# First loads of a gated mix of linear attention and a SwiGLU network: one weight piece moved to another queue, another held behind a memset, and the tables of GpSimd cut into tasks

## The chip, the core and the metric

The kernel runs on one core of a Trainium2 chip. The metric is the device time of one execution in microseconds (us); the median of several runs is given with their lowest and highest. A profiled execution has a time of its own and a span, which is the stretch from the first to the last recorded instruction.

## What is computed

For 2048 tokens of width 640 (bf16), a linear attention with 32 heads of width 20 and a SwiGLU network of width 1728 are computed from the same x and mixed by a gate for each token:

```python
g = sigmoid((x * gate_w).sum(-1, keepdims=True))
q, k, v = split_heads(x @ wqkv)                  # 32 heads of 20
pq, pk  = q @ w_phi[h], k @ w_phi[h]
phi     = concat(softmax(p), softmax(-p))        # for q and for k, 40 wide
kv, z   = phi_k^T v, sum of phi_k over tokens
a       = (phi_q kv) / (phi_q z + 1e-6) @ wo
b       = (silu(x @ w_gate) * (x @ w_up)) @ w_down
out     = g * a + (1 - g) * b
```

## The kernel before

The tokens are handled in four blocks of 512 (bt) and 16 tiles of 128 (t). x is loaded transposed into xT, five column blocks of 128 each. The SwiGLU width is cut into 14 pieces k of 128: for a block and a k, five matmuls with w_gate and five with w_up fill two PSUM banks ("gate", "up"); ACT takes a tanh of the first into hT and a copy of the second into one of three us buffers, DVE combines, and POOL multiplies hT by us ("hmul"), which frees the us buffer. w_phi is folded into the weights of q and k: POOL builds a block diagonal table wbd from w_phi (build_wbd, lines 507 to 519: five times a copy and two selects), PE multiplies wqT by wbd ("pre", premult, line 692), and ACT copies the result to wqk ("prev"). POOL also builds a mask kvm (build_mask, lines 521 to 532), which the kv sums need much later.

The order of work isn't written out by hand. Each piece of work is a task with an engine, a cost, dependences and a rank (prio); class _Plan (line 225) runs a small clock and, whenever an engine is free, emits the task with the lowest rank whose dependences are met. A transfer has a due time written in the source (land), and tasks that need it are emitted after this time. So due times set the order in which each engine's instructions stand, and the engines keep that order: an instruction that waits holds up those behind it. Real waits are on semaphores that the tracker (line 33) places from overlaps of reads and writes. A transfer waits only for what it reads and writes in SBUF, and is issued in the order of its engine's list.

The head (ffn_head, line 602) is the first real work of PE: after nine warm-up matmuls on zeros (warm, line 537) it computes k = 0 and k = 1 of block 0 side by side, 20 matmuls in four bank halves. It goes by column blocks of x (0 and 1, then 2, 3, 4), each with w_gate and then with w_up, so that it can start when the first columns are there. Behind it come k = 2 and 3 of block 0, then k = 0, 1, 2 of block 1, then the five premultiplies for k's weights.

The first transfers: on SP's list x's first block in four transposing transfers (line 476), then w_gate and w_up columns 256 to 511 (load_gu, line 449), x's second block, and so on through all weights (lines 479 to 493); on ACT's list w_gate and w_up columns 0 to 255 (lines 477, 478), behind the load of the activation table and a tanh of one element; on POOL's list w_phi (line 473). Small memsets of DVE (zeros for the warm-up, ones in v for the denominators, zero rows of hT and wd) are at lines 498 to 505. All matmuls carry line 395, all activations line 405, transfers line 423.

Of the kernel before, what the change touches and what calls it, by code (L numbers as in the profile page):

```python
# [6 lines left out]
P = 128  # L7
S_TOK = 2048
D = 640
# [289 lines left out]
def _build(  # L299
# [116 lines left out]

    out_evs = []

    def dma(eng, dst, src, transpose=False, keep=False):
        eobj = tr.engobj[eng]  # L420
        reads = [src] if src.tensor.name in tr.addr else []
        writes = [dst] if dst.tensor.name in tr.addr else []
        fn = (lambda: eobj.dma_start(dst, src, transpose=True)) if transpose else (lambda: eobj.dma_start(dst, src))
        ev = run(eng, fn, reads=reads, writes=writes, semname="dma")
        if keep:
            out_evs.append(ev)

    chain = {}  # L430

    def load(eng, dst, src, land, prio, transpose=False, name="load", cost=0.06):

        t = add(eng, cost, lambda: dma(eng, dst, src, transpose=transpose), prio=prio, lat=2.0, name=name)
        t.land = land
        t.after = chain.get(eng)
        chain[eng] = t
        return t

    def rows(a):  # L440
        return a.rearrange("(c p) j -> p c j", p=P)
# [12 lines left out]
    def load_x(bt, prio, *cuts):  # L454

        tok = slice(512 * bt, 512 * bt + 512)
        out_ = []
        for i, (c0, c1, land) in enumerate(cuts):
            out_ += [load("sp", xT[:, c0:c1, tok], x2[tok, c0 * P:c1 * P], land, prio + 0.1 * i, True, "x%d" % bt)] * (c1 - c0)
        return out_  # L460
# [7 lines left out]
    def load_gate():  # L468
        with nc.allow_non_contiguous_dma(reason="gate_w column load (640 elems)"):
            dma("act", wvg[:, :, D:D + 1], gate_ap)  # L470
    gw_l = add("act", 0.5, load_gate, prio=-7, lat=6.0, name="gw")
    gw_l.hold = 11.0
    ph_l = load("pool", wph[:, :, :], rows(A_w_phi.rearrange("h e f -> (h e) f")), 6.0, -20, cost=0.9)

    xs = [None] * NBT
    xs[0] = load_x(0, -42, (0, 2, 4.2), (2, 3, 6.7), (3, 4, 7.3), (4, 5, 7.8))
    wgl[0] = load("act", wg[:, :, 0:256], gsrc[:, :, 0:256], 5.1, -19, cost=0.5)
    wul[0] = load("act", wu[:, :, 0:256], usrc[:, :, 0:256], 6.2, -18, cost=0.5)
    load_gu(1, "sp", (8.9, 10.0), -37)
    xs[1] = load_x(1, -36, (0, 5, 13.2))  # L480
    load_gu(2, "sp", (15.0, 16.2), -35)
    wkT_l = load_wT(1, 19.2, -34)
    load_gu(3, "sp", (22.6, 24.5), -33)
    wv_l = load("sp", wvg[:, :, 0:D], rows(A_wqkv[:, 2 * D:3 * D]), 28.6, -32)
    xs[2] = load_x(2, -31, (0, 5, 30.5))
    load_gu(4, "sp", (32.4, 34.3), -30)
    wgl[NPC] = load("sp", wg[:, :, 1664:1728], gsrc[:, :, 1664:1728], 33.8, -29)
    wul[NPC] = load("sp", wg[:, :, 1728:1792], usrc[:, :, 1664:1728], 34.1, -28)
    xs[3] = load_x(3, -27, (0, 5, 38.0))
    wqT_l = load_wT(0, 41.5, -26)  # L490
    wd_l = [load("sp", wd[:, 0:13, :], rows(B_w_down[0:13 * P, :]), 52.0, -25),
            load("sp", wd[0:64, 13, :], B_w_down[13 * P:F_FFN, :], 53.0, -24)]
    wo_l = load("sp", wo[:, :, :], rows(A_wo), 56.0, -23)
    xl = [x_[4] for x_ in xs]

    zero = add("dve", 0.3, lambda: memset(us[:, 0, :], 0.0, "dve"), prio=-20, name="zero")
    table = add("act", 1.3, lambda: actop(us[:, 1, 0:1], us[:, 0, 0:1], ACTF.Tanh), deps=[zero], prio=-20, name="table")
    wgl[0].deps.append(table)  # L500
    v1ones = v1[:, :, :].rearrange("p t (h d) -> p t h d", d=DH + 1)[:, :, :, DH:DH + 1]
    ones_t = add("dve", 0.4, lambda: memset(v1ones, 1.0, "dve"), prio=-19)
    add("dve", 1.0, lambda: memset(hT[64:P, :, 13, :], 0.0, "dve"), prio=-18)
    wdz = add("dve", 0.7, lambda: memset(wd[64:P, 13, :], 0.0, "dve"), prio=-18)
    wd_l[1].deps.append(wdz)

    def build_wbd():
        for c in range(5):
            nh = PHI_NH[c]
            d_ = wbd[:, c, 0:nh, :]  # L510
            s_ = wph[:, c, :].unsqueeze(1).to_broadcast([P, nh, DH])
            poolop(lambda d_=d_, s_=s_: pool.tensor_copy(d_, s_), [wph[:, c, :]], [d_])
            poolop(lambda d_=d_, c=c, nh=nh: pool.affine_select(
                out=d_, in_=d_, pattern=[[-DH, nh], [0, DH]], compare_op=ALU.is_ge, fill=0.0,
                base=P * c - DH * PHI_H0[c], channel_multiplier=1), [d_], [d_])
            poolop(lambda d_=d_, c=c, nh=nh: pool.affine_select(
                out=d_, in_=d_, pattern=[[DH, nh], [0, DH]], compare_op=ALU.is_gt, fill=0.0,
                base=DH * PHI_H0[c] + DH - P * c, channel_multiplier=-1), [d_], [d_])
    wbd_t = add("pool", 6.0, build_wbd, deps=[ph_l], prio=-5, name="wbd")

    def build_mask():
        memset(kvm[:, :, :], 0.0, "pool")
        for g in range(5):
            d_ = kvm[:, g, :].rearrange("p (k d) -> p k d", d=DH + 1)
            memset(d_, 1.0, "pool")
            poolop(lambda d_=d_, g=g: pool.affine_select(
                out=d_, in_=d_, pattern=[[-2 * DH, 4], [0, DH + 1]], compare_op=ALU.is_ge, fill=0.0,
                base=P * g - 2 * DH * WHEAD[g], channel_multiplier=1), [d_], [d_])
            poolop(lambda d_=d_, g=g: pool.affine_select(
                out=d_, in_=d_, pattern=[[2 * DH, 4], [0, DH + 1]], compare_op=ALU.is_gt, fill=0.0,  # L530
                base=2 * DH * WHEAD[g] + 2 * DH - P * g, channel_multiplier=-1), [d_], [d_])
    mask_t = add("pool", 5.0, build_mask, prio=-6, name="mask")


    wctx = {}
# [66 lines left out]
    def ffn_head():  # L602
        tsl = slice(0, 512)
        cs = [{}, {}]
        before = warm_t
        lasts = [None, None]
        for c0, c1 in ((0, 2), (2, 3), (3, 4), (4, 5)):
            for j, (w, wl) in enumerate(((wg, wgl), (wu, wul))):
                def fn(c0=c0, c1=c1, j=j, w=w):
                    mms([(bank(cs[k]["ps"], j, 0, 512), w[:, c, P * k:P * k + P], xT[:, c, tsl], c == 0, c == 4)  # L610
                         for c in range(c0, c1) for k in range(2)])
                last = add("pe", _mm(*[512] * (2 * (c1 - c0))), fn, deps=[xs[0][c1 - 1], wl[0]], prio=-5,
                           acq=[("ps", cs[0], "ps"), ("ps", cs[1], "ps")] if c0 == 0 and j == 0 else (), name="head")
                last.after = before
                before = last
                lasts[j] = last
        for k in range(2):
            ffn_tail(0, k, cs[k], lasts, 0)

# [72 lines left out]
    def premult(which, wT_l, prio, step=0.0, at=0.0):  # L692
        ev = []
        for m in range(5):
            ctx = {}

            def fn(m=m, ctx=ctx):
                i = ctx["ps"]
                l = [wqT[:, 5 * which + c, P * m:P * m + P] for c in range(5)]

                def r(c, k0, k1):
                    return wbd[:, c, k0:k1, :].rearrange("p k f -> p (k f)")
                mms([(bank(i, 0, 0, 140), l[0], r(0, 0, 7), True, False),
                     (bank(i, 0, 120, 260), l[1], r(1, 0, 7), False, False),
                     (bank(i, 0, 240, 320), l[2], r(2, 0, 4), False, True),
                     (bank(i, 1, 0, 80), l[2], r(2, 4, 8), True, False),
                     (bank(i, 1, 60, 200), l[3], r(3, 0, 7), False, False),
                     (bank(i, 1, 180, 320), l[4], r(4, 0, 7), False, True)])
            t1 = add("pe", 0.4, fn, deps=[wT_l, wbd_t], prio=prio + step * m, acq=[("ps", ctx, "ps")], name="pre")
            t1.hold = at + 1.1 * m if at else 0.0  # L710

            def ev_fn(m=m, ctx=ctx):
                i_ = wide(ctx["ps"], 1024).rearrange("p (b x) -> p b x", b=2)[:, :, 0:320]
                o_ = wqk[:, which, m, :].rearrange("p (b x) -> p b x", b=2)
                actop(o_, i_, ACTF.Copy)
            ev.append(add("act", 0.6, ev_fn, deps=[t1], prio=-1, rel=[("ps", ctx, "ps")], name="prev"))
        return ev
# [102 lines left out]
    def kvpart(bt, half, prio):  # L820
# [28 lines left out]
        if bt == NBT - 1:  # L849
            ks = kvsb[:, half, :, :].rearrange("p g w -> p (g w)")  # L850
            km = kvm[:, :, :].rearrange("p g w -> p (g w)")
            kvs_t[half] = add("dve", 0.75, lambda: dveop(lambda: dve.tensor_tensor(ks, ka, km, ALU.mult), [ka, km], [ks]),
                              deps=[e_, mask_t], prio=1.4, name="kvs")
    kva_t = {}
    kvs_t = {}

# [134 lines left out]
```

## Time and profile before

| | |
|---|---|
| median of 3 runs | 292.27 us (291.34 to 293.55) |
| profiled execution | 292.22 us, span 290.5 us |
| PE busy | 282.6 us |
| DVE busy | 218.3 us |
| POOL busy | 165.3 us |
| ACT busy | 146.3 us |
| granted TensorE clock | 1.00 |

Times in the profile count from the start of the span. An engine's name with a q (SPq, ACTq) is its queue of instructions, here the issue of transfers; the number behind the start is how long the issue took, not the transfer. In square brackets stands how long the engine was idle before, and what released it. "x4" are four instructions merged into a row; PE's matmuls overlap, so a row's length is from the first start to the last end. In the list of waits, a row gives the sum of the waits, their number and the longest.

### The profile page before, as it was taken

How to read it: one execution, taken by the hardware profiler on the slowest of the kernel's cores; microseconds unless marked ns; L12 is line 12 of the kernel's file. 1: busy time of each engine (PE TensorE's matmuls, PEld its weight loads, DVE VectorE, ACT ScalarE, POOL GpSimd, SP SyncE). 2: the span in 40 equal slices, each digit the busy share in tenths (PEclk: the TensorE clock that was granted, in tenths of full speed). 3: DMA queues.
4: the chain of work that ended last, by engine and by line, in shares of the span. 5: the costliest groups of instructions: out<-in, count | busy, mean ns of one | idle time of the engine just before them, and what ended most of it. 6: DMA issues, size and time to landing. Idle time of an engine off the chain costs nothing.

```text
span 290.5 us, 5068 instructions
## 1 busy us (share of the span) xinstructions
PE 282.6 (97%) x1980; PEld 152.8 (53%) x2017; DVE 218.3 (75%) x323; ACT 146.3 (50%) x216; POOL 165.3 (57%) x136
## 2 busy tenths in 40 slices
PE   6899999999999999999999999999999999999996
PEld 2345555555555456556555556554556554554554
DVE  1232979999999998978998895899997879641022
ACT  2457567656746644443455335555663554654200
POOL 7764164763964686455647555767886546644300
PEclk9999999999999999999999999999999999999999
DMA  7999998000000000000326553434433543121021
GB/s 152 248 238 319 246 262 271 2 2 2 0 0 2 0 2 0 2 0 14 73 49 95 113 63 75 115 69 90 85 76 71 90 93 68 21 54 20 23 70 45
DMA packets 62776, 23.38 MB, mean 80 GB/s; under 512 B 51280, under 2 KB 62752, under 8 KB 62752
## 3 DMA queue, kind: packets, MB, share of 16 engines
q1 hardware_dynamic: 60752, 22.37, 34.7%
q10 hardware_dynamic: 1968, 0.66, 1.2%
q8 instruction: 16, 0.26, 0.4%
q14 instruction: 8, 0.07, 0.1%
q0 software_dynamic: 32, 0.03, 0.0%
HBM read 8.30 MB, written 2.62 MB: 38 GB/s over the span
## 4 chain that ended last, share of the span: by engine, by line
PE 95%; DMA 2%; issue 1%; ACT 1%; DVE 0%
PE ps L395 95%; DMA wu<-in_B_w_up_dram 2%; ACT L405 0%; ACT wqk L405 0%; ACT us L405 0%; DVE xsb L651 0%
## 5 line engine op out<-in xcount | busy, mean ns | idle before, releaser
L809 POOL TENSOR_TENSOR phi<-phi,rc 128x1280 bf16<-128x1280 bf16 x32 | 75.8, 2368 | 53.4 <-DVE rc L803 53.4
L579 POOL TENSOR_TENSOR hT<-hT,us 128x512 bf16<-128x512 bf16 (+1 forms) x56 | 64.3, 1154 | 45.0 <-DVE hT L573 30.3
L395 PE MATMUL ps<-xT,wg 128*128 128x512 bf16 x266 | 67.0, 379 | 1.7 <-DMA xT<-in_A_x_dram 1.0
L395 PE MATMUL ps<-xT,wu 128*128 128x512 bf16 x260 | 64.9, 379 | 1.0 <-DMA wu<-in_B_w_up_dram 1.0
L395 PE MATMUL ps<-wd,hT 128*128 128x128 bf16 (+1 forms) x440 | 62.1, 298 | 0.4
L573 DVE SCALAR_TENSOR_TENSOR hT<-hT,ps 128x512 bf16<-128x512 bf16 (+1 forms) x56 | 37.8, 676 | 26.4 <-ACT hT L405 26.4
L405 ACT ACTIVATE hT<-ps 128x512 bf16<-128x512 f32 (+1 forms) x56 | 33.4, 597 | 45.6 <-PE ps L395 45.3
L799 DVE TENSOR_REDUCE sm<-phi 128x64 f32<-128x1280 bf16 x32 | 47.3, 1479 | 11.5 <-ACT phi L405 11.5
L405 ACT ACTIVATE phi<-phi 128x1280 bf16<-128x1280 bf16 x32 | 40.6, 1269 | 21.5 <-DVE phi L789 21.2
L395 PEld LDWEIGHTS ps<-wd,hT 128*128 128x128 bf16 x448 | 35.0, 98 | 27.9
L395 PE MATMUL ps<-wqk,xT 128*128 128x128 bf16 (+1 forms) x311 | 47.4, 297 | 0.5
L405 ACT ACTIVATE us<-ps 128x512 bf16<-128x512 f32 (+1 forms) x56 | 33.3, 598 | 21.8 <-PE ps L395 21.6
L395 PEld LDWEIGHTS ps<-xT,wu 128*128 128x128 bf16 x260 | 25.3, 98 | 32.0 <-DMA wu<-in_B_w_up_dram 1.5
L395 PEld LDWEIGHTS ps<-xT,wg 128*128 128x128 bf16 x280 | 25.6, 98 | 26.3 <-DMA wg<-in_B_w_gate_dram 1.9
L395 PEld LDWEIGHTS ps<-wqk,xT 128*128 128x128 bf16 x320 | 26.4, 98 | 22.0
L777 DVE TENSOR_REDUCE mx<-ps 128x32 f32<-128x640 f32 x32 | 26.0, 811 | 7.7 <-PE ps L395 7.7
L781 DVE TENSOR_REDUCE mn<-ps 128x32 f32<-128x640 f32 x32 | 25.8, 808 | 0.0
L789 DVE TENSOR_TENSOR phi<-mn,ps 128x640 bf16<-128x640 f32 x32 | 25.7, 803 | 0.0
L785 DVE TENSOR_TENSOR phi<-ps,mx 128x640 bf16<-128x640 f32 x32 | 25.4, 795 | 0.0
L395 PE MATMUL ps<-wo,oT 128*128 128x128 bf16 (+1 forms) x158 | 23.7, 298 | 0.1
L395 PE MATMUL ps<-wvg,xT 128*128 128x129 bf16 (+1 forms) x156 | 22.6, 298 | 0.2
L665 POOL TENSOR_TENSOR xsb<-xsb,xb 128x640 bf16<-128x640 bf16 x12 | 16.7, 1396 | 9.1 <-ACT xb L405 9.1
(42 smaller groups left out, 174.8 us busy)
## 6 DMA issues: line engine op xcount, KB each, us to landing
out_dram<-xsb SPq DMA_DIRECT2D x15, 160.0 KB, 1.8
wd<-in_B_w_down_dram SPq DMA_DIRECT2D x1, 2080.0 KB, 9.8
wvg<-in_A_wqkv_dram SPq DMA_DIRECT2D x1, 800.0 KB, 7.6
wo<-in_A_wo_dram SPq DMA_DIRECT2D x1, 800.0 KB, 10.6
wg<-in_B_w_gate_dram SPq DMA_DIRECT2D x2, 320.0 KB, 4.2
wu<-in_B_w_up_dram SPq DMA_DIRECT2D x2, 320.0 KB, 4.9
wg<-in_B_w_gate_dram SPq DMA_DIRECT2D x1, 640.0 KB, 4.5
wu<-in_B_w_up_dram SPq DMA_DIRECT2D x1, 640.0 KB, 5.9
```

The costliest lines, as they stand in the source:

```text
L395: last = pe.matmul(o, lhsT=l, rhs=r, start=st, stop=sp_, skip_group_check=True)
L405: run("act", lambda: act.activation(o, i, func, scale=scale), reads=reads, writes=[o])
L573: dveop(lambda: dve.scalar_tensor_tensor(out=hap, in0=hap, scalar=1.0, in1=g_, op0=ALU.add, op1=ALU.mult), [hap, g_], [hap])
L579: poolop(lambda: pool.tensor_tensor(hap, hap, u_, ALU.mult), [hap, u_], [hap])
L665: poolop(lambda: pool.tensor_tensor(x_, x_, b_, ALU.add), [x_, b_], [x_])
L777: dveop(lambda: dve.tensor_reduce(a, b, AX.X, ALU.max), [b], [a])
L781: dveop(lambda: dve.tensor_reduce(a, b, AX.X, ALU.min), [b], [a])
L785: dveop(lambda: dve.tensor_tensor(o_, a, b, ALU.subtract), [a, mx[:, ctx["st"], :]], [o_])
L789: dveop(lambda: dve.tensor_tensor(o_, a, b, ALU.subtract), [b, mn[:, ctx["st"], :]], [o_])
L799: dveop(lambda: dve.tensor_reduce(a, b, AX.X, ALU.add), [b], [a])
L809: poolop(lambda: pool.tensor_tensor(a, a, b, ALU.mult), [a, r], [a])
```

## The change

Transfers: w_up columns 0 to 255 and w_phi move to SP's list; x's first block is loaded in two transfers (columns blocks 0 and 1, and 2 to 4) instead of four; w_gate columns 0 to 255 stay alone on ACT's list, and the transfer is entered as reading the ones of v, so that it waits for DVE's memset of them (behind). SP's list now begins: x blocks 0 and 1, x blocks 2 to 4, w_up 0 to 255, w_gate and w_up 256 to 511, w_phi, x's second block, and then as before. The due times of the loads are rewritten.

The head takes w_gate first, column blocks 0 and 1, then 2 to 4, and then ten matmuls with w_up over all five. The number of matmuls and their operands stay the same.

wbd and the mask become five tasks each, one for each of the five parts, with the same copy or memset and two selects; the memset of the whole mask to zero goes. The mask's rank falls from -6 to 3, but while POOL waits for w_phi's due time nothing else is ready, and all five parts of the mask stand ahead of wbd in POOL's list; all of wbd stands ahead of the first hmul, as before. With the new due times the order of the later tasks changes in places: the same groups, some exchanged with neighbours (on PE for example a v tile stands ahead of a gate and up pair, and some kv, num and down groups change places).

```diff
-    def dma(eng, dst, src, transpose=False, keep=False):
+    def dma(eng, dst, src, transpose=False, keep=False, behind=()):
+
         eobj = tr.engobj[eng]
-        reads = [src] if src.tensor.name in tr.addr else []
+        reads = ([src] if src.tensor.name in tr.addr else []) + list(behind)
...
-    ph_l = load("pool", wph[:, :, :], rows(A_w_phi.rearrange("h e f -> (h e) f")), 6.0, -20, cost=0.9)
-
     xs = [None] * NBT
-    xs[0] = load_x(0, -42, (0, 2, 4.2), (2, 3, 6.7), (3, 4, 7.3), (4, 5, 7.8))
-    wgl[0] = load("act", wg[:, :, 0:256], gsrc[:, :, 0:256], 5.1, -19, cost=0.5)
-    wul[0] = load("act", wu[:, :, 0:256], usrc[:, :, 0:256], 6.2, -18, cost=0.5)
-    load_gu(1, "sp", (8.9, 10.0), -37)
-    xs[1] = load_x(1, -36, (0, 5, 13.2))
-    load_gu(2, "sp", (15.0, 16.2), -35)
-    wkT_l = load_wT(1, 19.2, -34)
...
+    xs[0] = load_x(0, -42, (0, 2, 4.2), (2, 5, 7.0))
+    wgl[0] = add("act", 0.5, lambda: dma("act", wg[:, :, 0:256], gsrc[:, :, 0:256], behind=[v1ones]), prio=-19, name="load")
+    wgl[0].land = 5.4
+    wul[0] = load("sp", wu[:, :, 0:256], usrc[:, :, 0:256], 8.0, -39)
+    load_gu(1, "sp", (9.4, 10.5), -37)
+    ph_l = load("sp", wph[:, :, :], rows(A_w_phi.rearrange("h e f -> (h e) f")), 10.9, -36.5)
+    xs[1] = load_x(1, -36, (0, 5, 13.0))
+    load_gu(2, "sp", (15.0, 16.5), -35)
+    wkT_l = load_wT(1, 19.6, -34)
...
     ones_t = add("dve", 0.4, lambda: memset(v1ones, 1.0, "dve"), prio=-19)
+    wgl[0].deps += [table, ones_t]
...
-    wbd_t = add("pool", 6.0, build_wbd, deps=[ph_l], prio=-5, name="wbd")
-
-    def build_mask():
-        memset(kvm[:, :, :], 0.0, "pool")
-        for g in range(5):
...
-    mask_t = add("pool", 5.0, build_mask, prio=-6, name="mask")
...
+    wbd_t = [add("pool", 1.2, lambda c=c: build_wbd(c), deps=[ph_l], prio=-5, name="wbd") for c in range(5)]
+
+    def build_mask(g):
...
+    mask_t = [add("pool", 1.0, lambda g=g: build_mask(g), prio=3, name="mask") for g in range(5)]
...
-        lasts = [None, None]
-        for c0, c1 in ((0, 2), (2, 3), (3, 4), (4, 5)):
-            for j, (w, wl) in enumerate(((wg, wgl), (wu, wul))):
+        lasts = []
+        for j, (w, wl) in enumerate(((wg, wgl), (wu, wul))):
+            for c0, c1 in ((0, 2), (2, 5)) if j == 0 else ((0, 5),):
...
-                lasts[j] = last
+            lasts.append(last)
...
-            t1 = add("pe", 0.4, fn, deps=[wT_l, wbd_t], prio=prio + step * m, acq=[("ps", ctx, "ps")], name="pre")
+            t1 = add("pe", 0.4, fn, deps=[wT_l] + wbd_t, prio=prio + step * m, acq=[("ps", ctx, "ps")], name="pre")
```

The other due times that change lie 0.5 to 3.4 us earlier (w_v 28.6 to 26.3, x's fourth block 38.0 to 36.8, w_o 56.0 to 52.6, for example), but for w_up columns 512 to 767 and w_k, which lie 0.3 and 0.4 later.

More of the change, by code (lines that the diff above doesn't have):

```diff
@@ L426, in dma @@
             out_evs.append(ev)
+    v1ones = v1[:, :, :].rearrange("p t (h d) -> p t h d", d=DH + 1)[:, :, :, DH:DH + 1]
     chain = {}
@@ L482, in _build @@
-    wkT_l = load_wT(1, 19.2, -34)
[L483 to L492, printed above, removed]
@@ L493, in _build @@
-    wo_l = load("sp", wo[:, :, :], rows(A_wo), 56.0, -23)
+    xs[0] = load_x(0, -42, (0, 2, 4.2), (2, 5, 7.0))
[5 more added lines that the diff above has]
+    xs[1] = load_x(1, -36, (0, 5, 13.0))
@@ new lines, in _build @@
+    load_gu(2, "sp", (15.0, 16.5), -35)
+    wkT_l = load_wT(1, 19.6, -34)
+    load_gu(3, "sp", (22.0, 24.0), -33)
+    wv_l = load("sp", wvg[:, :, 0:D], rows(A_wqkv[:, 2 * D:3 * D]), 26.3, -32)
+    xs[2] = load_x(2, -31, (0, 5, 30.1))
+    load_gu(4, "sp", (31.5, 33.0), -30)
+    wgl[NPC] = load("sp", wg[:, :, 1664:1728], gsrc[:, :, 1664:1728], 33.4, -29)
+    wul[NPC] = load("sp", wg[:, :, 1728:1792], usrc[:, :, 1664:1728], 33.8, -28)
+    xs[3] = load_x(3, -27, (0, 5, 36.8))
+    wqT_l = load_wT(0, 40.4, -26)
@@ L494, in _build @@
+    wd_l = [load("sp", wd[:, 0:13, :], rows(B_w_down[0:13 * P, :]), 50.2, -25),
+            load("sp", wd[0:64, 13, :], B_w_down[13 * P:F_FFN, :], 50.6, -24)]
+    wo_l = load("sp", wo[:, :, :], rows(A_wo), 52.6, -23)
     xl = [x_[4] for x_ in xs]
@@ L499, in _build @@
     table = add("act", 1.3, lambda: actop(us[:, 1, 0:1], us[:, 0, 0:1], ACTF.Tanh), deps=[zero], prio=-20, name="table")
-    wgl[0].deps.append(table)
-    v1ones = v1[:, :, :].rearrange("p t (h d) -> p t h d", d=DH + 1)[:, :, :, DH:DH + 1]
     ones_t = add("dve", 0.4, lambda: memset(v1ones, 1.0, "dve"), prio=-19)
+    wgl[0].deps += [table, ones_t]
     add("dve", 1.0, lambda: memset(hT[64:P, :, 13, :], 0.0, "dve"), prio=-18)
@@ L505, in _build @@
     wd_l[1].deps.append(wdz)
[L507 to L518, printed above, removed]
@@ L519, in _build @@
-    wbd_t = add("pool", 6.0, build_wbd, deps=[ph_l], prio=-5, name="wbd")
-    def build_mask():
-        memset(kvm[:, :, :], 0.0, "pool")
-        for g in range(5):
[L524 to L531, printed above, removed]
@@ L532, in _build, with build_wbd @@
-    mask_t = add("pool", 5.0, build_mask, prio=-6, name="mask")
+    def build_wbd(c):
+        nh = PHI_NH[c]
+        d_ = wbd[:, c, 0:nh, :]
+        s_ = wph[:, c, :].unsqueeze(1).to_broadcast([P, nh, DH])
+        poolop(lambda: pool.tensor_copy(d_, s_), [wph[:, c, :]], [d_])
+        poolop(lambda: pool.affine_select(
+            out=d_, in_=d_, pattern=[[-DH, nh], [0, DH]], compare_op=ALU.is_ge, fill=0.0,
+            base=P * c - DH * PHI_H0[c], channel_multiplier=1), [d_], [d_])
+        poolop(lambda: pool.affine_select(
+            out=d_, in_=d_, pattern=[[DH, nh], [0, DH]], compare_op=ALU.is_gt, fill=0.0,
+            base=DH * PHI_H0[c] + DH - P * c, channel_multiplier=-1), [d_], [d_])
@@ new lines, in _build @@
+    wbd_t = [add("pool", 1.2, lambda c=c: build_wbd(c), deps=[ph_l], prio=-5, name="wbd") for c in range(5)]
+    def build_mask(g):
+        d_ = kvm[:, g, :].rearrange("p (k d) -> p k d", d=DH + 1)
+        memset(d_, 1.0, "pool")
+        poolop(lambda: pool.affine_select(
+            out=d_, in_=d_, pattern=[[-2 * DH, 4], [0, DH + 1]], compare_op=ALU.is_ge, fill=0.0,
+            base=P * g - 2 * DH * WHEAD[g], channel_multiplier=1), [d_], [d_])
+        poolop(lambda: pool.affine_select(
+            out=d_, in_=d_, pattern=[[2 * DH, 4], [0, DH + 1]], compare_op=ALU.is_gt, fill=0.0,
+            base=2 * DH * WHEAD[g] + 2 * DH - P * g, channel_multiplier=-1), [d_], [d_])
@@ L852, in kvpart @@
             kvs_t[half] = add("dve", 0.75, lambda: dveop(lambda: dve.tensor_tensor(ks, ka, km, ALU.mult), [ka, km], [ks]),
-                              deps=[e_, mask_t], prio=1.4, name="kvs")
+                              deps=[e_] + mask_t, prio=1.4, name="kvs")
     kva_t = {}
```

## The prediction

> **What bounds the kernel now.** I read the page first (engine shares), then the waits of PE, then the chain of work, then the timeline of the first 25 us, then the DMA view of the first 13 us.
>
> ```profile
> span 290.5 us, 5068 instructions
> ...
> PE 282.6 (97%) x1980; PEld 152.8 (53%) x2017; DVE 218.3 (75%) x323; ACT 146.3 (50%) x216; POOL 165.3 (57%) x136
> ```
>
> PE is busy 97% of the span, so only an earlier start of its work, or fewer holes in it, can shorten the kernel. The list of waits holds these holes for PE and no others:
>
> ```profile
> PE ps L395 <- DVE us L415: 1.3, 1, 1.3
> ...
> PE ps L395 <- DMA xT<-in_A_x_dram: 1.0, 1, 1.0
> PE ps L395 <- DMA wu<-in_B_w_up_dram: 1.0, 1, 1.0
> ...
> PE ps L395 <- ACT wqk L405: 0.4, 1, 0.4
> ```
>
> The 1.3 is the start. The two of 1.0 stand in the head (the first 20 real matmuls), the 0.4 in the premultiply. From 24.12 to 288.27 us PE is busy for 262.21 of 264.15 us: nothing is left to gain there. The timeline of the head:
>
> ```profile
> 0.81 5.26 SPq L423 DMA_TRANSPOSE xT<-in_A_x_dram  x4
> ...
> 1.25 0.45 ACTq L423 DMA_DIRECT2D wg<-in_B_w_gate_dram  x1
> ...
> 1.26 4.02 PE L395 MATMUL ps<-us 128*128 128x512 bf16 x9 [1.26 <-DVE us L415]
> ...
> 1.73 0.55 ACTq L423 DMA_DIRECT2D wu<-in_B_w_up_dram  x1
> ...
> 2.08 0.27 DVE L415 MEMSET v<- 128x256 bf16 x1 [0.87 <-issue]
> ...
> 6.32 1.02 PE L395 MATMUL ps<-xT,wg 128*128 128x512 bf16 x4 [1.04 <-DMA xT<-in_A_x_dram]
> ...
> 8.33 1.04 PE L395 MATMUL ps<-xT,wu 128*128 128x512 bf16 x4 [0.98 <-DMA wu<-in_B_w_up_dram]
> ...
> 11.79 1.24 PE L395 MATMUL ps<-xT,wg 128*128 128x512 bf16 x5
> ```
>
> The warm-up ends at 5.28, four matmuls run at 6.32, then PE waits for w_up's first piece (issued at 1.73 on ACT's queue, landed 6.6 later, at 8.3). From 8.33 the other 16 matmuls of the head run without a wait (16 x 0.216 = 3.46), and the next group starts at 11.79. Everything behind that is a chain of PE, so I forecast this one start, call it T (11.79 now): what T moves, the end moves. The most there is to win: with no wait at all T = 5.28 + 20 x 0.216 = 9.6, a gain of 2.2 us.
>
> **The landings before**, from the DMA view asked at each issue, are issue plus time to landing: x columns 0-1 0.81 + 5.4 = 6.2; x blocks 2, 3, 4 at 8.6, 8.8 and 9.3; w_gate piece 0 1.25 + 4.6 = 5.85; w_up piece 0 8.3; w_gate piece 1 (SP, right behind x) 6.12 + 4.3 = 10.4. The rate that they had:
>
> ```profile
> GB/s 0 0 0 0 0 0 10 188 137 95 174 259 328 325 341 207 137 128 288 267 196 232 203 137 86 291 286 246 293 290 293 290 288 269 290 290 290 290 290 290
> ```
>
> Each figure is 0.325 us. From 8.1 us on the 16 engines hold about 290 GB/s; before that the rate dips twice (137, 128 at 5.2 to 5.85; 137, 86 at 7.5 to 8.1).
>
> **The change, part by part.**
>
> SyncE's list. Four transposes become two. Their issues took 1.35 us (two column blocks) and 1.25 (one block each); I take 1.45 for three blocks, 0.1 a block; the only large one near, five blocks while the engines are full, took 4.15, which is the other end. So SP is at w_up's first piece at 0.81 + 1.35 + 1.45 + two gaps of 0.06 = 3.7, at w_gate's second at 4.3, w_up's second at 5.0, w_phi at 5.8, x's second block at 6.4 (7.55 before). SP's issuing costs nothing itself: the transfers behind it are limited by bytes, and later loads had no PE wait.
>
> w_up piece 0 is issued 2.0 us later but queues behind x alone. The bytes ahead of it and its own are x block 0 (0.655 MB), w_gate piece 0 (0.328) and itself (0.328): 1.31 MB. Summing the GB/s line, 1.31 MB had moved by 8.45 us, and 0.98 MB (x and w_gate) by 6.8. Between last byte and landing lie 0.7 us: the first 1.66 MB, which end with w_gate piece 1, had moved at 9.7, and that piece landed at 10.4. So x's second part lands at 7.5 and w_up at 9.15. Ends: at 290 GB/s from the first byte, 6.4 and 7.5; if w_up simply inherits the landing of w_gate piece 1, whose place in SP's list it takes, 10.4. I take 9.15, the row measured on these very bytes.
>
> w_gate piece 0 now waits for the memset of v's ones, which ends at 2.35 (2.08 + 0.27): issue 2.40 instead of 1.25. Nothing is queued behind it on ACT until the first tanh (11.56 before). By its old landing time it is there at 7.0, by the shortest for this size in the trace (4.1) at 6.5; I take 6.8, since w_up no longer shares the engines with it.
>
> The head on PE. Ten w_gate matmuls, then ten of w_up, instead of pairs by column block. Four start at 6.8 and end at 7.65, x's rest is there at 7.5, the other six end at 8.95; w_up is there at 9.15; ten matmuls of 0.216 give T = 9.2 + 2.16 = 11.35. With w_gate at 6.5 and w_up before 8.66, T = 6.5 + 20 x 0.216 = 10.8; with w_up at 10.4, T = 12.6. I take 11.2, between the first two and nearer to the measured rate: a gain of 0.6 us.
>
> w_phi and GpSimd. POOL loses one DMA issue (1.02) and one memset (some 0.5), both off the path; the mask is built at once in its first 5 us. But w_phi now lands sixth on SP's queue: two more pieces of 0.328 MB at 290 GB/s behind w_up (8.45 + 2.26 = 10.7), 0.7 to land, 0.4 for its own small rows (0.1 by bytes, and 1.0 as upper end): W = 11.8, where it was there before POOL asked at 7.0. The five tables keep their 15 instructions, and they stay ahead of the products hT:
>
> ```profile
> 7.03 0.30 POOL L512 COPY wbd<-wph 128x140 bf16<-128x140 bf16 x1
> ...
> 12.18 0.34 POOL L516 TENSOR_SCALAR_AFFINE_SELECT wbd<-wbd 128x140 bf16<-128x140 bf16 x1
> ...
> 13.29 3.38 POOL L579 TENSOR_TENSOR hT<-hT,us 128x512 bf16<-128x512 bf16 x3 [0.77 <-ACT us L405]
> ...
> 23.28 3.08 ACT L405 ACTIVATE wqk<-ps 128x640 bf16<-128x640 f32 x5
> ...
> 24.12 0.79 PE L395 MATMUL ps<-wbd,wqT 128*128 128x140 bf16 x12 [0.43 <-ACT wqk L405]
> ```
>
> Tables take 12.52 - 7.03 = 5.5, then POOL works off the products, 1.13 each. Each frees one of three us buffers, and ACT, in its order, needs the fourth product before its seventh us copy (0.60), which stands ahead of the first wqk copy (0.62), which PE's fourth premultiply awaits. Together W + 5.5 + 4.5 + 0.6 + 0.6 + some 0.45 of handing over and one tanh = W + 11.65. Unhindered, that premultiply comes at T + 12.33 (24.12 - 11.79). So POOL stalls PE only when W is later than T + 0.7 = 11.9. At 11.8 it just clears: cost 0, but each us of delay costs one.
>
> The rest of PE's order changes (v tiles a little earlier, pairs exchanged). w_v landed at 27.1 and the first v group would now be wanted near 27.8; no PE wait after 24.12 was longer than 0.4. I take 0, ends 0 and 0.4 a case. The tail behind 288.27 (2.2 us) has the same instructions: 0.
>
> Sum: profiled execution 292.22 (span 290.5 and 1.7 around it; the median of the runs is 292.27) - 0.6 = 291.6.
>
> **Rivals.**
>
> First, w_up is late (slower). It is issued 3.7 - 1.73 = 2.0 us later; with its old 6.6 to landing it is there at 10.3, T = 12.5, time 292.9. It decides from a landing after 9.6. For it: its place is that of a piece that landed at 10.4. Against: that piece had w_up's own bytes and w_phi's ahead of it. [...] Chance 0.15.
>
> Second, W is late (slower). If w_phi lands 7.6 us after its issue, as w_v did, W is 13.4 and the end 1.5 later than mine, 293.1; with the 10.8 that x block 2 took, 296. Chance 0.15.
>
> Third, PE loses its pace. The nine warm-up matmuls ran at 0.43 each, those of the head at 0.216. If the longer wait for w_gate and x set them back, 20 x 0.21 = 4.2 us are lost: 295.8. Against: PE was busy for just 1.03 of the 3.05 us to 8.33 and stayed fast. [...] Chance 0.03.
>
> Fourth, the gain is lost again to new small waits behind the reordered body: 292.2. Chance 0.12.
>
> **How the numbers follow.** Forecast (T 10.4 to 11.6, so 290.8 to 292.0; 10.4 were w_gate there at 6.1) 0.55; the four rivals 0.45. The range 290.2 to 293.5 takes in the T of 10.8 (291.2) less the scatter of the runs below their median (292.27 - 291.34 = 0.9), the first and fourth rivals, and half of the second. About 1% (2.9 us) is what a measurement of this kernel can tell from no change. Faster by more would take more than the 2.2 us that the head holds: 0.02. Slower by more needs the third rival or the far end of the second: 0.07. Within 1%: 0.91.
>
> **What would show it.** PE's wait for wu after the warm-up below 0.5 us and the third group at 11.2 (10.8 to 11.6); the ACT issue of wg at 2.4; w_phi's first POOL copy near 11.8 and no PE wait for wqk over 0.5 us; PE's waits after 25 us still under 0.5 in all. I am wrong in the step on bytes if w_up lands after 9.6, in the step on W if POOL's first copy comes after 12, and in the cover of the body if PE shows holes behind 25 us.

## The result and the profile after

The changed kernel takes 296.11 us (median of 6 runs, 294.18 to 297.59), the kernel before 292.61 us in the runs beside it. The ratio is 1.0122, 95% interval 1.0073 to 1.017: slower by 1.2%. The forecast was 291.6 us, with a range of 290.2 to 293.5.

The profiled execution of the changed kernel took 296.21 us. From here on lines carry the numbers of its own source (two fewer behind the mask, one more at the transfers). The page:

```profile
span 294.5 us, 5073 instructions
...
PE 285.0 (97%) x1980; PEld 153.1 (52%) x2017; DVE 221.3 (75%) x323; ACT 145.6 (49%) x216; POOL 163.3 (55%) x134
```

The span is 4.0 us longer and PE still 97% busy: part of the loss is busy time, 2.4 us more for the same 1980 matmuls. The timeline of the head, changed kernel:

```profile
0.80 2.92 SPq L424 DMA_TRANSPOSE xT<-in_A_x_dram  x2
...
2.38 0.44 ACTq L424 DMA_DIRECT2D wg<-in_B_w_gate_dram  x1
...
3.77 0.58 SPq L424 DMA_DIRECT2D wu<-in_B_w_up_dram  x1
...
7.26 4.12 PE L395 MATMUL ps<-xT,wg 128*128 128x512 bf16 x10 [1.99 <-DMA wg<-in_B_w_gate_dram]
...
11.21 2.32 PE L395 MATMUL ps<-xT,wu 128*128 128x512 bf16 x10
...
11.56 0.30 POOL L512 COPY wbd<-wph 128x140 bf16<-128x140 bf16 x1 [6.57 <-DMA wph<-in_A_w_phi_dram]
...
13.37 1.24 PE L395 MATMUL ps<-xT,wg 128*128 128x512 bf16 x5
...
25.70 0.79 PE L395 MATMUL ps<-wbd,wqT 128*128 128x140 bf16 x12 [0.43 <-ACT wqk L405]
```

Two rows of ten equal matmuls stand one below the other, the first with 4.12 us, the second with 2.32. The start of the first row ran at half pace, after PE had sat idle from 5.28 to 7.26. Two rows from narrower windows show the turn within the first ten, two matmuls in 1.06 us and two in 0.59:

```profile
7.66 1.06 PE L395 MATMUL ps<-xT,wg 128*128 128x512 bf16 x2
10.78 0.59 PE L395 MATMUL ps<-xT,wg 128*128 128x512 bf16 x2
```

The starts of the ten lie about 0.43 us apart up to 10.53 (with one pause, from 8.52 to 9.30) and 0.21 to 0.25 from there: seven to eight of them were slow. So the third group starts at T = 13.37, against 11.79 before: 1.58 of the 4.0 us. The rest, from T to the end of the span, is 294.5 - 13.37 = 281.1, against 290.5 - 11.79 = 278.7: the other 2.4 us lie behind the head. PE's waits of the changed kernel between 100 and 220 us, where the kernel before shows none:

```profile
PE ps L395 <- DMA eT<-phi: 0.6, 1, 0.6
PE ps L395 <- DMA oT<-ob: 0.4, 1, 0.4
PE ps L395 <- DVE phi L787: 0.3, 1, 0.3
```

and one of these places in its timeline:

```profile
191.21 1.35 SPq L424 DMA_TRANSPOSE eT<-phi  x1
...
196.33 0.56 PE L395 MATMUL ps<-kvsb,eT 128*128 128x84 bf16 x10 [0.60 <-DMA eT<-phi]
```

The num group stands in PE's list where its transposed features are not there yet: they were issued at 191.21 and land after 196. The three rows are less than the 2.4 us. From T to the end PE is busy for 275.06 us, against 274.06 before, so 1.4 of the 2.4 us are time in which PE stood idle, and 1.0 is longer busy time, which the waits don't list.

### The profile page after: what moved, and what is told of

The parts are those of the page before. It is cut to its first block, busy times and chain, and to the rows that moved or that the text cites. A ratio compares the mean times of both kernels' runs of the same rounds, so it can differ in the third digit from the quotient of the medians.

```text
span 294.5 us, 5073 instructions
## 1 busy us (share of the span) xinstructions
PE 285.0 (97%) x1980; PEld 153.1 (52%) x2017; DVE 221.3 (75%) x323; ACT 145.6 (49%) x216; POOL 163.3 (55%) x134
## 4 chain that ended last, share of the span: by engine, by line
PE 74%; DVE 15%; DMA 5%; ACT 2%; issue 2%; POOL 0%; DVEq 0%
PE ps L395 74%; DVE sm L797 3%; DVE mx L775 2%; DMA oT<-ob 2%; DVE phi L787 2%; DVE mn L779 2%; DMA eT<-phi 2%; DVE phi L783 2%; ACT phi L405 2%; DMA wg<-in_B_w_gate_dram 2%; DVE hT L571 2%; DVE rc L801 1%; DVE ob L887 1%; DVE kvacc L844 1%; DVE kvsb L850 1%
## 5 line engine op out<-in xcount | busy, mean ns | idle before, releaser
L395 PEld LDWEIGHTS ps<-xT,wg 128*128 128x128 bf16 x280 | 25.9, 99 | 28.6 <-DMA wg<-in_B_w_gate_dram 2.9
L395 PEld LDWEIGHTS ps<-wqk,xT 128*128 128x128 bf16 x320 | 26.3, 98 | 21.8 <-ACT xsb L405 0.3
L395 PE MATMUL ps<-wo,oT 128*128 128x512 bf16 (+1 forms) x157 | 23.9, 297 | 0.6 <-DMA oT<-ob 0.4
```

Source lines behind the costliest of these rows:

```text
L395: last = pe.matmul(o, lhsT=l, rhs=r, start=st, stop=sp_, skip_group_check=True)
```

## The experiments

Theory A was made from these two readings: one loss in the head, by half pace behind a longer idle time, and one behind it, by the exchanged order. All ratios are to the kernel before in runs on the same chip. T and "rest" (span minus T) are from one profiled execution each; a single rest scatters: kernels with the order of before behind the head have rests from 278.6 to 279.6, and up to 280.5 in e6 and e10. So the ratios decide. The profiled run can lie at an end of a kernel's runs: e3's was its fastest (293.08 us), those of e6 (293.62) and e7 (293.42) were their slowest.

| kernel | ratio, 95% interval | T | rest |
|---|---|---|---|
| changed kernel | 1.0122 (1.0073 to 1.017) | 13.37 | 281.1 |
| e1 changed, order of before | 1.0083 (1.0052 to 1.0114) | 13.59 | 279.0 |
| e2 before, order of changed | 1.0031 (1.0003 to 1.0058) | 10.97 | 280.9 |
| e3 changed, 16 warm-up matmuls | 1.0049 (1.0032 to 1.0066) | 11.81 | 279.6 |
| e4 changed, early w_gate | 1.0022 (0.9996 to 1.0048) | 11.45 | 280.9 |
| e5 before, 5 warm-up matmuls | 1.0029 (1.0007 to 1.0052) | 13.12 | 278.6 |
| e6 early w_gate, order of before | 1.0002 (0.998 to 1.0025) | 11.41 | 280.5 |
| e7 16 warm-up, order of before | 1.0011 (0.9993 to 1.003) | 12.13 | 279.6 |
| e8 before, w_gate behind the ones | 1.0068 (1.004 to 1.0096) | 13.47 | 279.0 |
| e9 before, 13 warm-up matmuls | 0.9966 (0.994 to 0.9993) | 10.93 | 279.2 |
| e10 e6 with 11 warm-up | 0.9993 (0.9968 to 1.0018) | 10.63 | 280.2 |
| e11 e3 in a third order | 1.0052 (1.0024 to 1.008) | 12.35 | 280.7 |
| e12 e10, w_phi on GpSimd's list | 0.9994 (0.9966 to 1.0021) | 11.41 | 278.7 |

### e1 and e2: the head and the order apart

Only due times differ. In e1 they are set so that behind the head every engine's list is that of the kernel before:

```diff
-    xs[0] = load_x(0, -42, (0, 2, 4.2), (2, 5, 7.0))
+    xs[0] = load_x(0, -42, (0, 2, 4.2), (2, 5, 5.9))
-    wul[0] = load("sp", wu[:, :, 0:256], usrc[:, :, 0:256], 8.0, -39)
+    wul[0] = load("sp", wu[:, :, 0:256], usrc[:, :, 0:256], 7.5, -39)
-    ph_l = load("sp", ..., 10.9, -36.5)
+    ph_l = load("sp", ..., 6.7, -36.5)
... (all others as in the kernel before)
```

In e2, the other way round, the kernel before has x's last column block due at 9.59, w_phi at 10.9 and all others as in the changed kernel.

> The changed kernel's transfers, head and tables, but due times under which everything behind the head stands in the order of the kernel before on every engine. Theory A (two losses: 1.6 us in the head from a late w_gate piece and ten matmuls at half pace, 2.3 us behind it from the new order): the third group starts at 13.4 as in the changed kernel, PE's holes behind 100 us are gone, span 292.1, time 293.8. Rival B (the order is innocent; the holes come from the later start and the moved transfers): holes of 1 us and more between 130 and 215 us stay, time 296.

> The kernel before with its transfers and its head, but due times under which everything behind the head stands in the order of the changed kernel on every engine. Theory A: third group at 11.8, holes of PE at about 135, 195 and 210 us of 2.3 us in all, time 294.6. Rival B: no such holes, 292.3 as before.

e1 measured 1.0083 (294.7 us), with T at 13.59; of PE's waits between 100 and 220 us, one of 0.2 us is left. e2 measured 1.0031, and its profile has the waits of the changed kernel (0.3 for phi at 135 us, 0.2 for oT at 209 us) with the transfers and the head of the kernel before; a further 0.7 us waits for w_v, wanted earlier. So the order costs by itself, and rival B falls; but 0.3 to 0.4%, about 1 us, not the 2.3 us that one pair of profiles showed. The wait for w_v is e2's own, the changed kernel has none, so e2 alone could put the order too high; e3 and e7 (below) show the same 0.4% without it. The head costs the larger part, 0.8%, 2.4 us.

### e3 and e4: the late piece and the pace

```diff
-        mms(acc(bank(wctx["ps"], 1, 0, 512), [(us[:, 0, 0:P], z)] * 9))
+        mms(acc(bank(wctx["ps"], 1, 0, 512), [(us[:, 0, 0:P], z)] * 16))
```

```diff
-    wgl[0] = add("act", 0.5, lambda: dma("act", ..., behind=[v1ones]), prio=-19, name="load")
+    wgl[0] = add("act", 0.5, lambda: dma("act", ...), prio=-19, name="load")
-    wgl[0].deps += [table, ones_t]
+    wgl[0].deps += [table]
```

The first is e3, the second e4; neither moves another instruction.

> The changed kernel with 16 warm-up matmuls on zeros in place of 9, in the same order. Theory A (PE fell to half pace in the hole between 5.28 and 7.26 us): the warm-up now reaches to about 7, the head's matmuls run at 0.216 each, the third group starts at 11.6 instead of 13.4, time 294.4. Rival C (half pace has another cause, such as the operands just landed, or the late w_gate piece is the whole loss): 0.43 each again for the first ten, third group at 13.4 or later, time 296.

> The changed kernel with w_gate's first piece issued at 1.25 again, not behind the memset of ones. Theory A: w_gate lands near 6.0, PE has no hole over 1.1 us before x's second part lands at about 8, no half pace, third group at 11.3 to 11.6, time 294.3. Rival D (x alone on the engines is what counts, an early w_gate slows x's first part by as much): x's first part at 6.2 again, x's rest at 8.5 or later, third group at 12 or later, time 295 or more.

The head of e3 in its timeline (the first row has 11 of the 16 matmuls on zeros):

```profile
3.37 3.71 PE L395 MATMUL ps<-us 128*128 128x512 bf16 x11
7.18 2.64 PE L395 MATMUL ps<-xT,wg 128*128 128x512 bf16 x10
9.66 2.32 PE L395 MATMUL ps<-xT,wu 128*128 128x512 bf16 x10
11.81 1.24 PE L395 MATMUL ps<-xT,wg 128*128 128x512 bf16 x5
```

w_gate is as late as in the changed kernel (7.18), and seven more matmuls on zeros bring T from 13.37 to 11.81 and the ratio from 1.0122 to 1.0049: 2.1 us by work that computes nothing. Rival C falls. At full pace the first ten take 2.64 us, not 2.32: the fifth starts 1.19 us after the first, where four matmuls take 0.86. That pause of 0.3 us stands in every kernel with the new head whose first four run at full pace (1.17 to 1.19 from first to fifth); what it waits for isn't settled (the views name x's transfer in e4 and nothing in e3). In e4 the first matmul comes at 5.98, all 20 run at full pace, T is 11.45. Rival D has a part of the truth: x's first part landed at 0.8 + 5.0 = 5.8, where it landed at 0.8 + 3.7 = 4.5 in the changed kernel. But PE was only waiting for w_gate there, and on time theory A is the nearer.

### e5 and e8: the same in the kernel before

```diff
-        mms(acc(bank(wctx["ps"], 1, 0, 512), [(us[:, 0, 0:P], z)] * 9))
+        mms(acc(bank(wctx["ps"], 1, 0, 512), [(us[:, 0, 0:P], z)] * 5))
```

e8 holds only w_gate's first piece of the kernel before behind the memset of ones, with w_up right behind it on ACT's list.

> The kernel before with 5 warm-up matmuls in place of 9, nothing else: four matmuls on zeros less, no transfer moved, so the clock by itself. Theory A (PE's pace falls or does not rise when it has little to do for some 3 us): the warm-up ends at 3.4, the head's first ten or more matmuls take 0.43 each, so the third group starts at 13.5 to 14 instead of 11.8 and the time is 1.7 to 2.2 longer, 294.3. Rival C (pace depends on something else, such as the late w_gate piece): the head runs at 0.216 as before, 292.4.

> The kernel before with only w_gate's first piece held behind the memset of ones (issue at 2.4, with w_up right behind it on ACT's list), everything else as it was. Theory A: first matmul near 7.2 instead of 6.3, a hole of 1.9 us behind the warm-up and half pace for part of the head, third group at 12.5 to 13.5, time 293.2 to 294. Rival F (the late w_gate piece hurts only with the new head that does ten w_gate matmuls first): third group at 11.8 to 12.2, 292.5.

The head of e5, where no transfer moved:

```profile
1.26 2.31 PE L395 MATMUL ps<-us 128*128 128x512 bf16 x5 [1.26 <-DVE us L415]
6.25 1.87 PE L395 MATMUL ps<-xT,wg 128*128 128x512 bf16 x4 [2.67 <-DMA xT<-in_A_x_dram]
7.90 1.91 PE L395 MATMUL ps<-xT,wu 128*128 128x512 bf16 x4
...
13.12 1.24 PE L395 MATMUL ps<-xT,wg 128*128 128x512 bf16 x5
```

Four matmuls take 1.87 us, where the kernel before took 1.02 for them, and T is 13.12. Over the runs it costs 0.29%, 0.8 us, less than the 1.7 to 2.2 expected; against e9, which is free of half pace (below), it is 1.0029 / 0.9966 = 1.0063, 1.8 us. So the kernel before seems to have half pace in some of its own runs. e8 costs 0.68%, 2.0 us: the wait for the memset alone, in the old head and the old order, makes most of the loss of the changed kernel. Rival F falls.

```profile
7.21 1.04 PE L395 MATMUL ps<-xT,wg 128*128 128x512 bf16 x4 [1.93 <-DMA wg<-in_B_w_gate_dram]
8.32 1.61 PE L395 MATMUL ps<-xT,wu 128*128 128x512 bf16 x4
9.72 1.06 PE L395 MATMUL ps<-xT,wg 128*128 128x512 bf16 x2
...
12.17 0.60 PE L395 MATMUL ps<-xT,wu 128*128 128x512 bf16 x2
```

This is the head of e8. The first four matmuls are fast (1.04), those from about 8.6 slow (1.06 for two), those from 12.2 fast again. So PE had its full pace and lost it in the middle of work, and e1 shows the same. Below its head stand two stretches of e1 and one of the kernel before: from where to where, the length, PE's busy time and, third from the end, the granted clock.

```profile
7.32 1.04 PE L395 MATMUL ps<-xT,wg 128*128 128x512 bf16 x4 [2.11 <-DMA wg<-in_B_w_gate_dram]
8.51 2.72 PE L395 MATMUL ps<-xT,wg 128*128 128x512 bf16 x6
11.02 2.73 PE L395 MATMUL ps<-xT,wu 128*128 128x512 bf16 x10
...
5.02:8.43 3.41, 1.23 (x5) 1.00 1.19 292
8.43:11.84 3.41, 3.33 (x8) 0.50 1.27 257
...
5.68:9.09 3.41, 1.78 (x8) 1.00 1.28 220
```

The clock shows this fall: 0.50 from 8.43 to 11.84 in e1, and from 8.64 to 12.05 in e8, each 3.41 us long. The traces of these kernels also record when the clock had turned to full: at 5.02 in e1, 5.23 in e8 and 5.68 in the kernel before. In the first 3.41 us from there PE was busy for 1.23 us (e1) and 1.41 us (e8), and the clock fell; with 1.78 us (the kernel before) it held, as it did with 2.3 us and more in e3, e7, e9, e10 and e11.

The profile of the changed kernel, like that of e5, has no record of the clock, and its slow matmuls seem to be another case: the nine on zeros are 0.43 us apart to the last, and so is the head from its first matmul. A turn to full pace and back between 5.1 and 7.26 would be shorter than the stretches recorded in e1 and e8 (3.41 us each), so by an estimate from these two PE had not turned to full pace at all before 10.6. Theory A's "PE fell to half pace in the hole" fits neither case to the letter: in e1 PE fell behind four fast matmuls, and here it seems not to have been fast before. Work on zeros in the hole helps against both: 16 warm-up matmuls bring the changed kernel from 1.0122 to 1.0049 (e3) and e1 from 1.0083 to 1.0011 (e7).

In e1 and e8 the slow matmuls do not stand right behind the idle time: PE had waited 2.11 and 1.93 us for w_gate, the four matmuls after that took 1.04 us in both, and the clock read 0.50 only from 8.43 (e1) and 8.64 (e8) on. The 3.41 us ahead of the fall held 1.23 and 1.41 us of matmuls: the fall came behind little work, not behind none. What decides it, the runs do not show beyond that.

### e6, e7, e9 and e10: both losses away

e6 and e7 are e1 with the edit of e4 or of e3; e10 is e6 with 11 warm-up matmuls. e9 is the kernel before with 13:

```diff
-        mms(acc(bank(wctx["ps"], 1, 0, 512), [(us[:, 0, 0:P], z)] * 9))
+        mms(acc(bank(wctx["ps"], 1, 0, 512), [(us[:, 0, 0:P], z)] * 13))
```

> The changed kernel with w_gate's first piece issued at 1.25 and the order of the kernel before behind the head: both losses taken away, the moved transfers and the head's new order kept. Theory A: third group at 11.3 to 11.5, no hole over 0.5 us behind 25 us, time 0.3 to 0.5 below the kernel before, 291.9. Rival E (the moved transfers cost something of their own behind the head): 293 or more, with a hole of PE that neither kernel shows.

> The changed kernel with 16 warm-up matmuls and the order of the kernel before behind the head; w_gate still behind the memset. Theory A: third group at 11.6 to 11.8, no half pace in any run, time as before, 292.1 to 292.4. Rival E: 293 or more.

> The kernel before with 13 warm-up matmuls in place of 9 and nothing else: they fill the hole of 1.04 us between 5.28 and the first real matmul at 6.3. Theory A: the first real matmul stays at 6.2 to 6.4 (x's first part decides), the pace is 0.216 in every run, and what the kernel before loses in runs in which its own head falls to half pace is gone: median 0 to 0.5 us below the kernel before, the highest runs lower. Rival H (the head of the kernel before never falls to half pace): the same within 0.1%.

> The changed kernel with w_gate's first piece issued at 1.25, 11 warm-up matmuls and the order of the kernel before behind the head. Theory A: third group at 11.2 to 11.5, no half pace, 291.8 to 292.3, so as the kernel before or 0.2% below. If it stays at 292.4 like the same kernel with 9, half pace was no part of that one's time, and its earlier third group is given back behind the head.

e6 (292.36 us) and e7 (292.63) are level with the kernel before: with half pace and the order taken back, the moved transfers, the head's new order and the late tables win nothing. e10 has the earliest third group of all (10.63) and is level too (292.55); its rest is 280.2, with a wait of 0.4 for oT at 191 us. A start earlier by some tenths is not passed on.

e9 is faster than both kernels: 291.64 us, ratio 0.9966. Its 12 runs lie between 291.33 and 292.83, the 29 of the kernel before beside it between 291.27 and 295.1. The lowest times are the same; the long ones are gone. The clock of the single runs says so too: one stretch of 3.41 us at 0.50 makes a mean of 0.994 over a run (1 - 1.7 / 292.6 in the profiled run of e1, which is listed with 0.994), and 12 of the 105 runs of the kernel before beside the experiments have that mean (293.2 to 294.8 us), as have 3 of 6 of the changed kernel, 4 of 6 of e1, 4 of 5 of e8 and none of e9's. It is a lower count, since a run without a record reads 1.00. Rival H falls.

```profile
1.26 4.44 PE L395 MATMUL ps<-us 128*128 128x512 bf16 x13 [1.26 <-DVE us L415]
6.18 1.02 PE L395 MATMUL ps<-xT,wg 128*128 128x512 bf16 x4 [0.47 <-DMA xT<-in_A_x_dram]
```

Thirteen warm-up matmuls took 4.44 us here where nine took 4.02: the last five already ran at full pace.

e9 is also the better kernel to compare with, since none of its runs shows half pace. e10's runs lie beside e9's on the same chip, and all twelve lie above e9's median: 0.9 us more by the medians, with a third group that starts 0.3 earlier. So what is kept in e10 of the change does cost something, which a comparison with the kernel before hides, since half pace lengthens some of its own runs. A part of it is in e10's profile:

```profile
17.67 0.60 ACT L405 ACTIVATE us<-ps 128x512 bf16<-128x512 f32 x1 [3.01 <-POOL hT L577]
...
17.10 1.24 PE L395 MATMUL ps<-xT,wg 128*128 128x512 bf16 x5
18.41 0.81 PE L395 MATMUL ps<-xT,wu 128*128 128x512 bf16 x3
```

ACT's us copy waits 3.01 us for POOL's products, which stand behind the late tables, and the groups of PE start 1.31 us apart instead of 1.08. From T to the first premultiply PE takes 11.22 us in e10 and 11.14 in e6, against 10.80 in the kernel before and 10.79 in e4, e9 and e12. So the late tables take back 0.4 of what the earlier start gives; the rest of the 0.9 us isn't traced.

### e11 and e12: what in the order costs

Set back of all due times only w_phi's and those of the head's loads, and the plan gives the order of before. Set back either alone, and it stays close to the changed order. So these due times exchange the groups together, and the many others don't; this is read from the plan, and no run here separates the two. e11 is e3 with w_v due at 28.6, which makes a third order, w_phi still late:

```diff
-    wv_l = load("sp", wvg[:, :, 0:D], rows(A_wqkv[:, 2 * D:3 * D]), 26.3, -32)
+    wv_l = load("sp", wvg[:, :, 0:D], rows(A_wqkv[:, 2 * D:3 * D]), 28.6, -32)
```

e12 is e10 with w_phi on GpSimd's list as in the kernel before, the mask's rank back at -6, and the same order behind the head:

```diff
-    ph_l = load("sp", ..., 6.7, -36.5)
+    ph_l = load("pool", ..., 6.7, -20, cost=0.9)
```

> The changed kernel with 16 warm-up matmuls and w_v's due time back at 28.6: behind the head the tasks fall into a third order, which is neither that of the kernel before nor that of the changed kernel. Theory G (the new order costs because w_phi's late due time puts GpSimd's tables later in the plan, which it still does here): 1.1 us over the same kernel in the old order, as in the new order, 293.6. Rival J (each order has small waits of its own, whatever the cause of the exchange): anything between 292.3 and 294.5, with PE's holes in other places than 135, 195 and 209 us.

> As the changed kernel with an early w_gate piece, 11 warm-up matmuls and the order of the kernel before, but w_phi on GpSimd's list again, so that its tables are ready by 13 and not by 17. Theory K (the late tables cost something behind the head, by products hT that come later): third group at 10.6 to 11.4, hole near 191 us gone, 291.6 like the kernel before with 13 warm-up matmuls. Rival L (the late tables are hidden; a start earlier than 11 is given back to waits for transposes in any case): 292.3 to 292.6, hole near 191 us still there.

e11 measured 1.0052, as e3 (1.0049) and not as e7 (1.0011), with waits of 0.6 for eT at 195 us and 0.3 for phi at 136 us, nearly the old places. That agrees with theory G, from one order more, but the tables are late in e7 as well, at no such cost: it is the order, not the lateness itself. e12 measured 0.9994, e10 0.9993, on different chips and with intervals of half a per cent: by time alone the late tables could be hidden (rival L). The profiles speak for theory K: e12 has a rest of 278.7, no wait at 191 us, and 10.79 us from T to the first premultiply, where e10 has 11.22. What the tables cost in time stays open, up to some tenths of a us.

## Why the prediction was wrong

**The transfers were forecast well.** SP reached w_up at 3.77 (forecast 3.7), w_gate was issued at 2.38 (2.40), x's rest landed at 2.2 + 5.5 = 7.7 (7.5), w_up at 3.77 + 5.1 = 8.9 (9.15; the first rival needed a landing after 9.6), POOL's first copy came at 11.56 (11.8). Further down SP's list the forecast ran early (w_phi was issued at 6.26 and not 5.8). On the path only w_gate's landing was off, 0.4 late (7.2 for 6.8): alone on ACT's queue it took 4.8, longer than the 4.6 it took with w_up behind it.

**The cover of w_phi was hardly tried.** PE's wait for wqk is 0.43 us, as before, and the second rival did not come. But that was luck: with T at 13.37 the limit T + 0.7 was 14.1, far above the 11.56 of the first copy. In e4, with T at 11.45 and the first copy at 11.70, the cover held in the order forecast. In the order of before it did not: e6 (T 11.41, copy 11.66) and e10 (10.63 and 10.99) lost 0.3 and 0.4 us to it, though both copies lie below T + 0.7.

**The step that failed first is "ten matmuls of 0.216".** From the first matmul at 7.26, the head at the pace of e3 (11.81 - 7.18 = 4.63 us, with the pause of 0.3, which the sum hadn't) would have given T = 11.9. It was 13.37, by half pace, 1.5 us. That was the third rival, with a chance of 0.03, and the reason against it was the mistake: "PE was busy for just 1.03 of the 3.05 us to 8.33 and stayed fast" is one execution, and its 3.05 us are not the 3.41 us behind the recorded turn of the clock, 5.68 to 9.09, which held 1.78 us. In e1 and e8 that stretch held 1.23 and 1.41 us, and the clock fell to 0.50 behind it; the spread of the kernel before (291.27 to 295.1, against 291.33 to 292.83 in e9) and the 12 of its 105 runs with a mean clock of 0.994 show that some of its own runs lost their pace too. The price of the rival was put too high: 4.2 us for 20 slow matmuls, where seven to thirteen were slow in the profiles.

**The second failure is "I take 0, ends 0 and 0.4 a case".** The order costs 0.6 to 1.1 us in four pairs (changed kernel and e1, e3 and e7, e2 and the kernel before, e4 and e6). It is the loss that the fourth rival named, at or above the 0.6 us put down for it. The profiles show waits of 0.2 to 0.7 us for phi, eT and oT in the new order, but that these make the loss isn't shown: kernels in the order of before have such waits as well (0.7 for eT in e7, 0.9 for oT in e6). That the kernel before had no wait behind 24.12 us was read as slack, and that was no ground for a cost of 0.

Together, 2.4 us of head (e1) and 0.9 of order (e2) give 3.3 of the measured 3.5 us (296.11 - 292.61).

**The gain of 0.6 us did not show.** w_up's wait did go, but the start of the first matmul moved from 6.32 to 7.26, and e6 and e10, with an early w_gate and a third group at 11.4 and 10.6, gain nothing measurable over the kernel before, though their intervals would still hold a gain of about 0.6 us. Against e9, e10 is slower. So "what T moves, the end moves" didn't hold for starts earlier than before.

## What to carry to other kernels

Fill the time up to the first real matmul with warm-up matmuls until the operands have landed, not for a fixed count: half pace cost 1.5 us in the head of the changed kernel, where the waits of PE behind it were 0.6 us and less, and 13 warm-up matmuls for nine brought the highest run of the kernel before from 295.1 to 292.83 us (e9). Read the spacing of matmuls when judging pace: a granted clock below 1 shows a loss and where it lies (0.50 from 8.43 to 11.84 in e1), but 1.00 can also mean that the profile has no record of it (the changed kernel and e5, with matmuls 0.43 us apart). Where a planner writes the order, a changed due time is a change of everything behind it: hold the order fixed in one kernel and change it alone in another before judging the transfer.

## What was not expected of the hardware

The granted clock is 1.00 in the profile of the changed kernel and of e5, where seven or eight and thirteen matmuls run at 0.43 us: these profiles have no record of the clock, and the views read that as 1.00. In e1 and e8, where the clock fell after it had risen, it reads 0.50 over just the slow stretch, 3.41 us. The turn to full pace came within the first nine warm-up matmuls or after them by the execution: the same first nine took 3.53 us in e6, 3.95 in e1 and 4.02 in the changed kernel. The recorded turns lie between 4.26 us (e9) and 5.74 (e3), so which matmuls fall into the 3.41 us behind the turn differs from run to run. PE was busy for 1.23 (e1) and 1.41 us (e8) of that stretch where the clock then fell, and for 1.78 us in the kernel before, where it held; whether this busy time decides, three executions do not show. Why the order that follows from the new due times fits worse stays open.
